# The two transfers that swap the halves of a pair's keys: begun by ScalarE behind its copy of the keys, or by SyncE in its line

## The chip, the cores and the metric

The kernel runs on one core of one Trainium2 chip. The metric is the device time of one execution in microseconds (us). Five engines matter here: TensorE (PE in the profile; PEld is its weight load), VectorE (DVE), ScalarE (ACT), GpSimd (POOL) and SyncE (SP, which issues transfers and computes nothing). Each works through its own instructions in order. A transfer (DMA) is begun by an instruction of one engine and carried out by DMA engines; a semaphore tells of its landing.

## What is computed

The reference is an attention with rotary positions, followed by a gated feed-forward layer and by a second one that chooses among eight experts. Only the attention is touched:

```python
def _attn_ref(q, k, v):                        # each 4 x 8 x 576 x 64, f32
    ...
    q_rot, k_rot = (rotate(q), rotate(k))
    scale = 1.0 / np.sqrt(D)
    scores = scale * np.matmul(q_rot, k_rot.transpose(0, 1, 3, 2))
    scores = scores - np.max(scores, axis=-1, keepdims=True)
    attn = np.exp(scores)
    attn = attn / (np.sum(attn, axis=-1, keepdims=True) + 1e-09)
    return np.matmul(attn, v).astype(np.float32)
...
x = attention, heads side by side: 2304 x 512
x = _moe_ref(x, ...)                           # (silu(x @ w_gate) * (x @ w_val)) @ w_out
return _moe2_ref(x, ...)                       # eight experts, one for each token, some tokens skipped
```

## The kernel before

The 32 heads are worked on as 16 pairs (0 to 15). A pair's queries are nine units of 128 rows (576 rows of two heads), so attention is 144 units, and one unit enters the pipeline in each step, or slot (`step`, L368). What a slot does stands in `ORDER`: the exponential of the unit before (`soft`, ScalarE), this unit's scores (`scores`, TensorE), part of an older unit's P.V product (`pv`), the copy of a finished product (`pv_out`, ScalarE, which also has SyncE store it to `xT`), the transposes of queries and keys of a coming pair (`qk_T`), the maximum (DVE), the transposes of the probabilities of the unit four slots back (`trans`), the jobs of this slot (`run_jobs`), and the copy of those transposed probabilities to SBUF (`his`: L282 on DVE for units 0, 2, 4, 6, L284 on ScalarE for the others).

The scores keep full f32 accuracy by splitting: of each number there is a high and a low part. `qk_T` transposes keys into the tile Ak, whose upper 64 partitions hold one part and whose lower 64 the other; ScalarE copies them out of PSUM in three groups (L186). The scores multiply Aq by Ak and by Bk, which is Ak with the two halves of its partitions exchanged. Bk is made in `swap` (L188): for pair 0 by TensorE, for the other 15 pairs by two transfers from SBUF to SBUF, 64 partitions of 4608 bytes each (L206, L207). The first product that reads Bk is the second matmul of the pair's unit 0 (L239).

When things are done is a table of slots relative to the pair's first unit (`AT`, `AT_FIRST`). The third group of keys is transposed and copied in slot -6 for pairs 2 to 15, and `swap` is a job of that same slot (for pair 1 it is slot -1). Slot -6 is the fourth slot of the pair before. In the slot's order the copy of the keys (L186) comes first, then the jobs with `swap`, then L284 for unit 8 of the pair before that one. In the next slot TensorE multiplies those probabilities by v (L318, `pv`), for which L284 must be done.

SyncE issues all other transfers of attention in the program's order, one after another: loads of q and k (L104), six loads of v (L116, L118), stores of x to `xT` (L337) and of the sums (L359). From slot 55 on it also issues, once per pair for eight pairs, what the next layer needs: a load of x (L560) and two to four loads of sums (L569). Weights for the next layer are loaded here and there (L457). The instructions' order on each engine is that of the program (`manual_schedule`), while the waits are put in by the framework.

Of the kernel before, what the change touches and what calls it, by code (L numbers as in the profile page):

```python
# [13 lines left out]
P = 128  # L14
G, R = 64, 9
# [3 lines left out]
def f32(ap):  # L19
    return ap.bitcast(F32)  # L20


class Attention:
# [164 lines left out]
    def swap(self, p):  # L188
        nc, st = self.nc, self.pairs[p]
        kb = self.p2.tile([P, 2 * S], F32R, tag="Bk", name=f"Bk_{p}")  # L190
        st["Bk"] = kb
        if p == 0:
            group = lambda t, g: t.rearrange("p (h r g) -> p h r g", h=2, r=R)[:, :, 3 * g:3 * g + 3]
            for g in range(3):
                if g < 2:
                    ps = self.psS.tile([P, 2, 512], F32, tag="S", name=f"swap{g}")[:, 0, :3 * P]
                else:
                    ps = self.psV.tile([P, 512], F32, tag="V", name=f"swap{g}")[:, :3 * P]
                ps = ps.rearrange("p (h r g) -> p h r g", h=2, r=3)
                nc.tensor.matmul(ps, self.swapr, group(st["Ak"], g), start=True, stop=True)  # L200
                if "b" + str(g) in self.FIRST_ON_DVE:
                    nc.vector.tensor_copy(group(kb, g), ps)
                else:
                    nc.scalar.copy(group(kb, g), ps)
            return
        nc.sync.dma_start(f32(kb[0:G]), f32(st["Ak"][G:P]))  # L206
        nc.sync.dma_start(f32(kb[G:P]), f32(st["Ak"][0:G]))  # L207

    def q_pad(self, p):
        nc, st = self.nc, self.pairs[p]  # L210
# [1292 lines left out]
```

## Time and profile before

| | before |
|---|---|
| median of 3 runs | 1042.92 us (1042.64 to 1045.4) |
| the profiled execution | 1042.63 us |
| its span in the trace | 1040.8 us |
| TensorE busy | 977.0 us (94%) |
| DVE busy | 559.6 us (54%) |
| ScalarE busy | 479.6 us (46%) |
| GpSimd busy | 442.4 us (43%) |

Attention takes roughly the first 330 us of the span. A share of the whole span says little about it, as ScalarE is far busier there than later; so the sums are read by stretch. In the timeline a row gives start, length, engine, line, operation and out<-in; in brackets stands the time for which the engine was idle before it, and what ended that. The rows of SyncE show the issuing instruction only, and not the transfer, which ends later. An x2 or x4 there is two or four issues in a row.

### The profile page before, as it was taken

How to read it: one execution, taken by the hardware profiler on the slowest of the kernel's cores; microseconds unless marked ns; L12 is line 12 of the kernel's file. 1: busy time of each engine (PE TensorE's matmuls, PEld its weight loads, DVE VectorE, ACT ScalarE, POOL GpSimd, SP SyncE). 2: the span in 40 equal slices, each digit the busy share in tenths (PEclk: the TensorE clock that was granted, in tenths of full speed). 3: DMA queues.
4: the chain of work that ended last, by engine and by line, in shares of the span. 5: the costliest groups of instructions: out<-in, count | busy, mean ns of one | idle time of the engine just before them, and what ended most of it. 6: DMA issues, size and time to landing. Idle time of an engine off the chain costs nothing. (4 is left out here: it accounts for less than half of the span.)

```text
span 1040.8 us, 16451 instructions
## 1 busy us (share of the span) xinstructions
PE 977.0 (94%) x5893; PEld 810.5 (78%) x5893; DVE 559.6 (54%) x962; ACT 479.6 (46%) x1041; POOL 442.4 (43%) x441
## 2 busy tenths in 40 slices
PE   5999998898989899999999999999999998998996
PEld 4787776676767878779999998999999876786643
DVE  6778776775856889883445233243245434225211
ACT  4888887786877333432343231232244314224232
POOL 6686777875830444455115315215216142112111
PEclk8999999998999999999999999999999999999999
DMA  5344455554532443413401211211222259506191
GB/s 175 91 135 126 134 154 146 148 137 130 126 85 101 140 122 101 121 57 92 137 23 54 77 46 31 76 47 31 73 89 62 72 139 395 223 31 215 32 371 57
DMA packets 81276, 119.80 MB, mean 115 GB/s; under 512 B 36469, under 2 KB 47365, under 8 KB 81168
## 3 DMA queue, kind: packets, MB, share of 16 engines
q1 hardware_dynamic: 77712, 110.01, 35.2%
q0 software_dynamic: 3456, 8.45, 2.8%
q8 instruction: 55, 0.90, 0.4%
q14 instruction: 53, 0.43, 0.1%
HBM read 87.73 MB, written 22.75 MB: 106 GB/s over the span
## 5 line engine op out<-in xcount | busy, mean ns | idle before, releaser
L614 POOL TENSOR_TENSOR hl<-h,hh 128x384 fp32r<-128x384 f32 x72 | 77.9, 1082 | 243.9 <-ACT hh L613 237.7
L251 DVE TENSOR_REDUCE nm<-S 128x1 f32<-128x576 f32 x144 | 108.3, 754 | 43.8 <-PE S L239 42.3
L259 ACT ACTIVATE P<-S,nm 128x576 f32<-128x576 f32 x144 | 107.2, 745 | 4.9 <-DVE nm L251 4.8
L613 ACT CAST hh<-h 128x384 fp32r<-128x384 f32 x72 | 37.0, 514 | 142.7 <-DVE h L612 142.7
L611 DVE TENSOR_TENSOR h<-g,h 128x384 f32<-128x384 f32 x72 | 40.0, 556 | 111.6 <-ACT h L610 111.6
L269 PE MATMUL T<-ident,P 128*128 128x128 f32 x576 | 90.9, 281 | 0.0
L239 PE MATMUL S<-Bk,Aq 128*128 128x288 f32 x256 | 74.5, 305 | 14.8 <-DMA Bk<-Ak 14.8
L627 PE MATMUL Y<-ohi,hl 128*128 128x512 f32 x216 | 85.9, 398 | 1.6 <-POOL hl L614 1.6
L318 PE MATMUL pv<-pt,rawv 128*64 128x384 f32 (+1 forms) x512 | 85.8, 438 | 1.5 <-ACT pt L284 1.4
L627 PE MATMUL Y<-ohi,hh 128*128 128x512 f32 x216 | 87.2, 404 | 0.0
L627 PE MATMUL Y<-olo,hh 128*128 128x512 f32 x216 | 85.3, 395 | 0.0
L239 PE MATMUL S<-Ak,Aq 128*128 128x288 f32 x256 | 83.0, 338 | 1.6 <-ACT P L259 1.6
L604 PE MATMUL g<-xa,ghi 128*128 128x384 f32 x216 | 75.6, 350 | 9.1 <-DVE h L611 8.6
L610 ACT ACTIVATE h<-g 128x384 f32<-128x384 f32 x72 | 35.1, 487 | 87.7 <-PE g L606 81.1
L606 PE MATMUL g<-xa,glo 128*128 128x384 f32 x216 | 72.4, 335 | 0.0
L606 PE MATMUL v<-xa,vlo 128*128 128x384 f32 x216 | 72.2, 334 | 0.0
L604 PE MATMUL v<-xa,vhi 128*128 128x384 f32 x216 | 72.1, 334 | 0.0
L269 PEld LDWEIGHTS T<-ident,P 128*128 128x128 f32 x576 | 64.6, 143 | 2.1 <-issue 1.2
L612 DVE TENSOR_TENSOR h<-v,h 128x384 f32<-128x384 f32 x72 | 40.2, 558 | 47.8 <-PE v L606 45.4
L239 PEld LDWEIGHTS S<-Bk,Aq 128*128 128x128 f32 x256 | 50.7, 198 | 16.6 <-issue 12.5
L282 DVE COPY pt<-T 128x512 f32<-128x512 f32 x64 | 44.2, 690 | 21.5 <-PE T L269 20.0
L239 PEld LDWEIGHTS S<-Ak,Aq 128*128 128x128 f32 x256 | 50.4, 197 | 6.7 <-issue 4.2
(268 smaller groups left out, 2533.3 us busy)
## 6 DMA issues: line engine op xcount, KB each, us to landing
wr_s<-in_moe_w_dram SPq DMA_DIRECT2D x46, 512.0 KB
xT<-x SPq DMA_DIRECT2D x32, 288.0 KB
x<-xT SPq DMA_DIRECT2D x24, 384.0 KB
Bk<-Ak SPq DMA_DIRECT2D x30, 288.0 KB
raw<-in_moe_w_gate_dram SPq DMA_DIRECT2D x12, 512.0 KB
raw<-in_moe_w_val_dram SPq DMA_DIRECT2D x12, 512.0 KB
raw<-in_moe_w_out_dram SPq DMA_DIRECT2D x12, 512.0 KB
wr<-in_moe_w_dram SPq DMA_DIRECT2D x10, 512.0 KB
```

The costliest lines, as they stand in the source:

```text
L239: nc.tensor.matmul(ps[:, c, :288], l, r[:, c * 288:(c + 1) * 288], start=(j == 0), stop=(j == len(ops) - 1))
L251: nc.vector.tensor_reduce(nm, st_u["S"], axis=AX.XY, op=ALU.max, negate=True)
L259: nc.scalar.activation(pt.rearrange("p (a b) -> p a b", a=2), st_u["S"], AF.Exp, bias=st_u["nm"], scale=1.0, accum_out=self.pairs[p]["l"][ ...
L269: nc.tensor.transpose(ps[:, kt * P:(kt + 1) * P], pt[:, kt * P:(kt + 1) * P], self.ident)
L282: self.nc.vector.tensor_copy(self.pt[:, :, cols], self.units[u]["T"])
L318: nc.tensor.matmul(ps[a * D:a * D + D, :n], st["raw"]["v"][:, h, 2 * third + a], self.pt[:, 2 * third + a, c0:c0 + n], start=(third == 0), ...
L604: nc.tensor.matmul(ps[m], wh[:, kt, cols], xh, start=(kt == 0), stop=False)
L606: nc.tensor.matmul(ps[m], wl[:, kt, cols], xh, start=False, stop=(kt == KT - 1))
L611: nc.vector.tensor_tensor(h, ps["g"], h, op=ALU.mult)
L612: nc.vector.tensor_tensor(h, ps["v"], h, op=ALU.mult)
L614: nc.gpsimd.tensor_tensor(hl, h, f32(hh), op=ALU.subtract)
L627: nc.tensor.matmul(self.acc[c][t], a[:, cols], b, start=(f == 0 and i == 0), stop=(f == FT - 1 and i == 2))
```

## The change

Both transfers that make Bk are issued by ScalarE and no longer by SyncE. Their place in the program, source, destination and size stay the same; for pair 0 nothing changes.

```diff
                 else:
                     nc.scalar.copy(group(kb, g), ps)
             return
-        nc.sync.dma_start(f32(kb[0:G]), f32(st["Ak"][G:P]))
-        nc.sync.dma_start(f32(kb[G:P]), f32(st["Ak"][0:G]))
+        nc.scalar.dma_start(f32(kb[0:G]), f32(st["Ak"][G:P]))
+        nc.scalar.dma_start(f32(kb[G:P]), f32(st["Ak"][0:G]))
```

## Rows read from the trace of the kernel before

**Rows 1.** Busy us (x instructions) by stretch, then PEclk, DMA share, GB/s:

```profile
52.40:143.40 91.00, 90.55 (x703) 70.02 (x701) 71.73 (x112) 77.94 (x193) 70.48 (x77) 1.00 0.51 135
143.40:310.80 167.40, 152.98 (x1121) 116.80 (x1122) 118.19 (x183) 125.41 (x310) 114.18 (x124) 0.95 0.49 131
```

**Rows 2.** Waits over the whole span: us in total, times, longest us:

```profile
PE S L239 <- DMA Bk<-Ak: 14.8, 6, 4.6
```

**Rows 3.** Timeline of TensorE: first products with Bk of pairs 12 and 14:

```profile
249.49 0.58 PE L239 MATMUL S<-Bk,Aq 128*128 128x288 f32 x1 [4.62 <-DMA Bk<-Ak]
...
291.20 0.37 PE L239 MATMUL S<-Bk,Aq 128*128 128x288 f32 x1 [2.77 <-DMA Bk<-Ak]
```

**Rows 4.** Timeline, pair 5: ScalarE's last copy of keys, and the swap:

```profile
95.33 0.48 ACT L186 CAST Ak<-M 128x384 fp32r<-128x384 f32 x1
...
95.84 0.54 SPq L206 DMA_DIRECT2D Bk<-Ak  x1
```

**Rows 5.** Timeline, pair 12: last copy of keys, and what follows:

```profile
233.48 0.48 ACT L186 CAST Ak<-M 128x384 fp32r<-128x384 f32 x1
233.89 0.59 ACT L284 COPY pt<-T 128x512 f32<-128x512 f32 x1
...
234.84 0.87 PE L318 MATMUL pv<-pt,rawv 128*64 128x384 f32 x4
```

**Rows 6.** Timeline of SyncE around the swap of pair 12, all issues:

```profile
221.92 0.54 SPq L337 DMA_DIRECT2D xT<-x  x1
222.56 2.14 SPq L457 DMA_DIRECT2D raw<-in_moe_w_val_dram  x1
225.38 0.33 SPq L104 DMA_DIRECT2D rawq<-in_q_dram  x1
225.81 1.36 SPq L116 DMA_DIRECT2D rawv<-in_v_dram  x2
227.22 1.27 SPq L118 DMA_DIRECT2D rawv<-in_v_dram  x1
228.53 2.78 SPq L116 DMA_DIRECT2D rawv<-in_v_dram  x2
232.72 0.59 SPq L118 DMA_DIRECT2D rawv<-in_v_dram  x1
234.69 0.38 SPq L560 DMA_DIRECT2D x<-xT  x1
235.39 2.79 SPq L569 DMA_DIRECT2D r<-rT  x4
238.28 0.55 SPq L337 DMA_DIRECT2D xT<-x  x1
238.94 0.42 SPq L359 DMA_DIRECT2D rT<-rr  x1
239.45 0.52 SPq L206 DMA_DIRECT2D Bk<-Ak  x1
240.02 0.59 SPq L207 DMA_DIRECT2D Bk<-Ak  x1
240.70 2.44 SPq L104 DMA_DIRECT2D rawk<-in_k_dram  x1
```

**Rows 7.** Waits of SyncE from 229 to 241 us, as rows 2:

```profile
SPq L118 <- DMA xT<-x: 1.4, 1, 1.4
SPq L560 <- DMA raw<-in_moe_w_val_dram: 1.3, 1, 1.3
...
SPq L569 <- DMA rawq<-in_q_dram: 0.3, 1, 0.3
```

**Rows 8.** Timeline: a copy by ScalarE, and TensorE that waited for it:

```profile
36.31 0.48 ACT L186 CAST Ak<-M 128x384 fp32r<-128x384 f32 x1 [0.40 <-PE M L177]
...
36.85 0.45 PE L177 MATMUL M<-identr,natk 128*128 128x128 f32 x3 [0.57 <-ACT Ak L186]
```

**Rows 9.** Timeline of POOL: the first work on the loaded x:

```profile
238.62 1.01 POOL L576 TENSOR_TENSOR x<-x 128x384 f32<-128x384 f32 x1 [5.10 <-DMA x<-xT]
```

## The prediction

> **What bounds the kernel now.** I read the sums by stretch first. In the stretch that covers five of attention's pairs without a long stall, TensorE is busy for 90.55 of 91.00 us, ScalarE for 77.94, at a granted clock of 1.00 [rows 1]: TensorE is the bound, and a pair costs 91.0 / 5 = 18.2 us. In the next eight pairs it is busy for 152.98 of 167.40 us at a clock of 0.95 [rows 1]: 14.4 us are idle, and the busy time is 153.0 - 8 x 18.1 = 8.2 us longer than at full clock. Then the list of waits: the one large wait of TensorE on a transfer is that of the scores for Bk, 14.8 us in six waits [rows 2]; the largest is 4.62 us, the last 2.77 us [rows 3]. All six lie at the first product of pairs 7, 8, 10, 11, 12 and 14. So there is something to win, but only in the second stretch.
>
> Why is Bk late there? Pair 5 shows the line as meant: ScalarE's copy of the keys ends at 95.33 + 0.48 = 95.81 and SyncE begins the first swap at 95.84 [rows 4]. In pair 12 the copy ends at 233.48 + 0.48 = 233.96 [rows 5], but SyncE comes to the swap at 239.45 only [rows 6], 5.5 us late; the second swap, begun at 240.02, lets TensorE go on at 249.49 [rows 3, 6], 9.5 us after its start. The reader is to see what held SyncE: at 232.72 a load of v waited 1.4 us for a store of xT, at 234.69 the load of x waited 1.3 us for a load of weights, at 235.39 the load of r waited for a load of q [rows 7]. These transfers share no data. Counting issues (x2 and x4 are two and four) shows the rule: each waits for the one eight places ahead of it. From the store at 221.92 to the load at 232.72, from the weights at 222.56 to x at 234.69, from q at 225.38 to the first r at 235.39 it is eight each time [rows 6]. Eight completion semaphores are handed out in turn, and a transfer doesn't start until the former owner of its semaphore has landed.
>
> **The change part by part.**
>
> *Removed: the wait for Bk.* Begun right behind the copy, the swap of pair 12 would start 5.5 us earlier, more than the stall of 4.62. If nothing holds it, all 14.8 us go [rows 2].
>
> *Added: two issues in ScalarE's order.* No issue by ScalarE stands in the trace; the nearest rows are the same two on SyncE: 0.57 us from the first's start to the second's (239.45 to 240.02), and 0.59 for the second, 1.16 in all [rows 6]. Behind them on ScalarE stands the copy of the transposed probabilities (L284), and for that TensorE waits with the P.V product L318. Today L284 starts at 233.89, 0.07 before the copy of the keys has ended, because nothing separates the two; it ends at 234.48, and L318 starts at 234.84, 0.36 later [rows 5]. This distance of 0.36 us stands at 13 of the 15 swaps. A released TensorE starts 0.06 after the copy's end (36.31 + 0.48 = 36.79, 36.85) [rows 8], which leaves 0.30 of slack. With the change L284 is later by 0.07 (lost overlap) + 0.03 (start behind the copy, as SyncE's in pair 5) + 1.16 = 1.26 us, so TensorE stalls 1.26 - 0.30 = 0.96 us per pair. That isn't made up, as TensorE is the bound there. Bounds: nothing, if ScalarE hands the issue on while it works; 0.46, if each takes the 0.33 of the cheapest load; and with a second issue held like the load of k behind the swaps today (2.44) [rows 6], 0.07 + 0.03 + 0.57 + 2.44 - 0.30 = 2.8. I take 0.96, the row of the same transfer.
>
> *Added: the turn of eight, now on ScalarE.* Nothing in the trace shows whether an issue by ScalarE keeps its place in that turn. The turn runs through every kind of SyncE's transfers without a break, so it goes by the program's order, not by tile or line; I take it that the swaps keep their places. Then the first swap of pair 12 waits for the eighth before it, the load of v issued at 232.72, and the second for the load of x issued at 234.69. The load of x ends a wait of POOL at 238.62 [rows 9], 3.9 us after its issue; by the same 3.9 (an estimate) the load of v lands at 236.6. ScalarE stands still from 233.96 to 238.6, issues the second swap, 0.59, and is free at 239.2. L284 comes 239.2 - 233.89 = 5.3 us later, TensorE stalls 5.3 - 0.3 = 5.0 us. Today's stall of this pair is 4.62. Queued behind the waiting instruction are L284 and then the next exponential, with DVE, POOL and TensorE behind these. So in the loaded stretch the stall moves from pair 12's first product to an L318 some ten us earlier, and is no shorter: the same line of SyncE (store of xT, load of v, load of x) sets both. For pairs 7 to 14 I put gain against cost at nothing, with bounds of -3 us (waits of ScalarE that come out shorter, as each delay gives SyncE's line time) and +6 us (0.96 in pairs 9 and 13, which have no stall today, and a place or two of the turn that is late in the others too).
>
> *Taken from SyncE:* two issues, 1.16 us a pair, and the load of k behind them can start earlier. TensorE waits for no other transfer [rows 2], so this is worth nothing directly.
>
> *Sum.* Pairs 1 to 6 and 15 have no stall to lose and pay 0.96 each: 7 x 0.96 = 6.7 us. Pairs 7 to 14: 0. The profiled run took 1042.63 us (span 1040.8), so 1042.6 + 6.7 = 1049.3 us; the profiled run is 0.3 under the median of 1042.92, so I leave it there. What follows attention begins with TensorE's last product and moves as a whole.
>
> **The rivals.**
>
> *The swaps are outside the turn of eight (faster).* If ScalarE's issues have semaphores of their own, it doesn't wait. The price is 15 x 0.96 = 14.4 us, the gain 14.8, and where the stalls go the clock need not fall: up to 8.2 us. 1042.6 + 14.4 - 14.8 - 8.2 = 1034.0 us. For it: the turn is seen on SyncE alone. Against it: it spares no kind of transfer. A rule of the Trainium skill bears on this side too (DMA: Bandwidth & Descriptors, "Queues, rings and completion order"): each issuing engine has rings of its own, and a DMA engine takes turns between rings. By it Bk would no longer stand behind the store of xT; the 9.5 us of pair 12 would shrink, and the same 14.8 us go, so it adds nothing to the sum. Chance 0.14.
>
> *ScalarE's issue is held (much slower).* Behind the swaps SyncE's load of k takes 2.44 us, the load of q of the same size 0.33 [rows 6]: something holds an issue for some 2 us when much is queued. If that hits the second swap on ScalarE, it adds 2.44 - 0.59 = 1.85 in each of the seven free pairs, 13 us: 1062 us; more if the loaded pairs pay as well. It decides from the point where SyncE's issues and ScalarE's meet. The Trainium skill has a rule for this (Perfetto Trace Analysis, "DMA Instruction — HWDGE"): the two issuing sequencers share one descriptor generator, locked for one issue at a time, and the lock wait counts in the instruction's time. Against it: the swaps themselves take 0.52 and 0.59 right behind the large store of xT [rows 6]. Chance 0.10.
>
> *Cheap issue, or an exchange that favours the change (even).* With 0.33 an issue the seven pairs cost 7 x 0.46 = 3.2 us; with the lower bound of the loaded pairs (-3) it is about nothing: 1042.6 to 1045.8, say 1043.5 us. Here falls also the case that the change does nothing: the swap starts no earlier and ScalarE has slack that I don't see. Chance 0.21.
>
> **How the numbers follow.** Forecast 1049.3 us, chance 0.55; its own range by the bounds above is 1042.6 + 3.7 to 1042.6 + 12.7, so 1046 to 1055. With the rivals the range is 1035 to 1060: it leaves out about half of each outer case. About 0.3%, 3.1 us, is what a measurement can tell here. Slower by more than that: 0.50 of the forecast and 0.10 of the held issue, 0.60. Same: 0.05 of the forecast and 0.17 of the even case, 0.22. Faster: 0.14 and 0.04 of the even case, 0.18.
>
> **What would show it.** Right: the 14.8 us of waits for Bk are gone; in their place L318 waits for ScalarE's L284, some 1 us in pairs 2 to 6 and 2 to 5 us in pairs 8, 10, 12 and 14; ScalarE's issues take 0.5 to 0.6 us, and in those pairs lie behind waits for a transfer of SyncE's. The period of pairs 2 to 6 goes from 18.1 to 19.1 us, that of the loaded ones stays near 21. Wrong: no wait of ScalarE on transfers (then the first rival, and a shorter second stretch), or issues of 2 us and more (the second), or L318 without a wait in pairs 2 to 6 (cheap issue).

## The result, and the profile after

The changed kernel takes 1054.55 us (median of 4 runs, 1052.12 to 1057.38) against 1042.78 us for the kernel before: a ratio of 1.011 with a 95% interval of 1.009 to 1.013. It is slower, as forecast, but by 11.8 us and not by 6.7. The profiled execution took 1057.38 us with a span of 1055.6 us, which is 14.8 us more than the span of before.

The page's busy times of after come first. TensorE is busy for about as long as before (979.7 us against 977.0), so 12.1 of the 14.8 us are idle time.

```profile
PE 979.7 (93%) x5893; PEld 812.8 (77%) x5893; DVE 558.5 (53%) x962; ACT 480.1 (45%) x1041; POOL 441.9 (42%) x441
```

The two stretches of [rows 1] follow, in the same columns (stretch, its length, busy us of PE, PEld, DVE, ACT and POOL with instructions, PEclk, DMA share, GB/s):

```profile
59.30:156.10 96.80, 90.65 (x703) 70.10 (x702) 71.16 (x111) 77.78 (x192) 69.81 (x77) 1.00 0.47 130
156.10:323.80 167.70, 150.57 (x1122) 115.40 (x1121) 119.88 (x184) 126.09 (x312) 115.46 (x124) 0.97 0.47 129
```

In the free stretch TensorE's work is the same (90.65 us against 90.55), and it lasts 5.8 us longer. In the loaded one 14.4 us of idle time became 17.1, the busy time fell by 2.4 us at the better clock (0.97 against 0.95), and the length stayed. TensorE's large waits in attention (20 to 330 us; total, times, longest) answer to [rows 2]:

```profile
PE pv L318 <- ACT pt L284: 23.9, 14, 3.4
PE S L239 <- DMA Bk<-Ak: 3.1, 1, 3.1
```

All six waits for Bk of before are gone, and fourteen waits of P.V for ScalarE's copy stand in their place, one in each of pairs 2 to 15. One wait for Bk is new. It is that of pair 1, which had none.

Every kernel below is read in the same way, by the start of the first product with Bk (L239, in the timeline of TensorE) of pairs 2, 7 and 15. The first column holds the start-up as well: TensorE's first matmul starts 9.8 (before) to 11.5 us (e12) into the span.

| kernel | until pair 2 | pair 2 to 7 | pair 7 to 15 | after that | span |
|---|---|---|---|---|---|
| before | 52.4 | 91.0 | 167.4 | 730.0 | 1040.8 |
| after | 59.3 | 96.8 | 167.7 | 731.8 | 1055.6 |
| after, again (e9) | 58.6 | 96.5 | 170.2 | 729.5 | 1054.8 |
| pair 1 by SyncE (e1) | 53.3 | 97.1 | 172.4 | 729.5 | 1052.2 |
| pair 1 by SyncE, again (e10) | 53.3 | 97.5 | 168.4 | 730.0 | 1049.2 |
| pair 1 at its copy (e8) | 54.0 | 96.5 | 169.0 | 729.2 | 1048.7 |
| behind L284 (e2) | 53.1 | 93.3 | 167.3 | 728.9 | 1042.6 |
| pairs 7 to 14 alone (e3) | 53.1 | 92.1 | 167.6 | 729.7 | 1042.5 |
| before, store split (e4) | 52.4 | 90.4 | 146.8 | 727.8 | 1017.4 |
| after, store split (e5) | 61.3 | 99.5 | 157.9 | 728.2 | 1046.9 |
| e1, store split (e6) | 53.3 | 97.5 | 156.0 | 732.1 | 1038.9 |
| e2, store split (e7) | 53.4 | 93.1 | 149.3 | 727.5 | 1023.3 |
| by GpSimd (e11) | 52.5 | 91.9 | 163.9 | 732.5 | 1040.9 |
| by GpSimd, store split (e12) | 53.2 | 90.4 | 146.8 | 730.4 | 1020.9 |

The first two lines say where the 14.8 us came from: 6.9 until pair 2 (0.8 of it a later first matmul, 10.57 us against 9.81), 5.8 to pair 7, 0.3 to pair 15 and 1.8 behind. The last is no more than what this column varies by (727.5 to 732.5).

**Pairs 2 to 6: the working of the prediction, seen.** The timeline of pair 5 (start, length, engine, line; in brackets the idle time before and what ended it) answers to [rows 4]:

```profile
104.91 0.48 ACT L186 CAST Ak<-M 128x384 fp32r<-128x384 f32 x1
...
105.42 0.47 ACTq L206 DMA_DIRECT2D Bk<-Ak  x1
...
105.93 0.61 ACTq L207 DMA_DIRECT2D Bk<-Ak  x1
...
106.58 0.59 ACT L284 COPY pt<-T 128x512 f32<-128x512 f32 x1 [1.19 <-PE S L239]
...
107.22 0.54 PE L318 MATMUL pv<-pt,rawv 128*64 128x384 f32 x2 [0.89 <-ACT pt L284]
```

The first issue starts 0.03 us behind the copy, the two take 0.47 and 0.61 us, and TensorE stalls 0.89 us. The releaser named for L284 had long been done; it is the two issues that fill the 1.19 us. In pair 4, which has a stall of 1.62 us, an issue waits as well:

```profile
85.17 0.49 ACT L186 CAST Ak<-M 128x384 fp32r<-128x384 f32 x1
86.42 0.47 ACTq L206 DMA_DIRECT2D Bk<-Ak  x1
86.93 0.61 ACTq L207 DMA_DIRECT2D Bk<-Ak  x1
87.58 0.59 ACT L284 COPY pt<-T 128x512 f32<-128x512 f32 x1 [1.92 <-DMA rawv<-in_v_dram]
```

The copy ends at 85.66 and the swap starts at 86.42. What let it go is the landing of a load of v: by its semaphore, SyncE's load begun at 79.42 landed at 86.35. Pair 6 is the same (begun at 118.16, landed at 125.14, stall 1.68 us).

**Pair 12: the wait on SyncE's transfers, seen.** ScalarE's rows answer to [rows 5], SyncE's to [rows 6]:

```profile
247.92 0.49 ACT L186 CAST Ak<-M 128x384 fp32r<-128x384 f32 x1
249.62 0.47 ACTq L206 DMA_DIRECT2D Bk<-Ak  x1
251.57 0.47 ACTq L207 DMA_DIRECT2D Bk<-Ak  x1
252.08 0.59 ACT L284 COPY pt<-T 128x512 f32<-128x512 f32 x1 [3.67 <-DMA r<-rT]
252.72 0.65 PE L318 MATMUL pv<-pt,rawv 128*64 128x384 f32 x2 [3.37 <-ACT pt L284]
...
243.19 1.79 SPq L116 DMA_DIRECT2D rawv<-in_v_dram  x2
246.78 0.60 SPq L118 DMA_DIRECT2D rawv<-in_v_dram  x1
248.09 0.39 SPq L560 DMA_DIRECT2D x<-xT  x1
248.78 2.85 SPq L569 DMA_DIRECT2D r<-rT  x4
```

The copy ends at 248.41. The first swap starts 1.2 us later, when the load of v begun at 243.19 has landed (249.55 by its semaphore), and the second another two us later, when the first of the loads of r has (251.55). Neither has any data in common with the swap; the wait is for the shared semaphore. In the trace SyncE's and ScalarE's transfers carry the same eight semaphores (100 to 107), and the two that ScalarE waited for had these two loads as owners. Over attention the list of waits (total, times, longest) gives ScalarE these, and the first line holds pairs 4 and 6 too:

```profile
ACT pt L284 <- DMA rawv<-in_v_dram: 9.3, 4, 2.8
ACT pt L284 <- DMA r<-rT: 3.7, 1, 3.7
ACT pt L284 <- DMA x<-xT: 1.8, 1, 1.8
```

**Pair 1: what the prediction missed.** Its last copy of keys and its swap:

```profile
27.23 0.48 ACT L186 CAST Ak<-M 128x384 fp32r<-128x384 f32 x1
...
31.82 0.51 ACTq L206 DMA_DIRECT2D Bk<-Ak  x1
32.36 0.60 ACTq L207 DMA_DIRECT2D Bk<-Ak  x1
...
36.56 0.38 PE L239 MATMUL S<-Bk,Aq 128*128 128x288 f32 x1 [3.11 <-DMA Bk<-Ak]
```

The copy ends at 27.71 and ScalarE comes to the swap 4.1 us later. For pair 1 the swap is a job of slot -1, while the last copy of keys lies in slot -3. SyncE, with nothing else to do, ran ahead to that job and waited for the copy alone: before, its swap started at 27.80. ScalarE has the slots between to work through. So Bk is 3.1 us late, just where the pipeline begins, and the clock falls behind the stall: between 36.5 and 48.0 us the granted clock is 0.70, a mixture of the 2.4 and the 1.2 GHz level (6.8 us at the lower one), against 1.00 in the same window of before.

### The profile page after: what moved, and what is told of

It reads as the page before. It is cut to its first block, busy times and chain, and to the rows that moved or that the text cites. A ratio compares the mean times of both kernels' runs of the same rounds, so it can differ in the third digit from the quotient of the medians.

```text
span 1055.6 us, 16380 instructions
## 1 busy us (share of the span) xinstructions
PE 979.7 (93%) x5893; PEld 812.8 (77%) x5893; DVE 558.5 (53%) x962; ACT 480.1 (45%) x1041; POOL 441.9 (42%) x441
## 5 line engine op out<-in xcount | busy, mean ns | idle before, releaser
L259 ACT ACTIVATE P<-S,nm 128x576 f32<-128x576 f32 x144 | 107.3, 745 | 7.9 <-DVE nm L251 6.9
L318 PE MATMUL pv<-pt,rawv 128*64 128x384 f32 (+1 forms) x512 | 85.0, 433 | 25.4 <-ACT pt L284 25.3
L239 PE MATMUL S<-Ak,Aq 128*128 128x288 f32 x256 | 82.8, 338 | 1.8 <-ACT P L259 1.5
L239 PE MATMUL S<-Bk,Aq 128*128 128x288 f32 x256 | 74.0, 303 | 3.1 <-DMA Bk<-Ak 3.1
L318 PEld LDWEIGHTS pv<-pt,rawv 128*64 128x64 f32 x512 | 28.6, 137 | 43.8 <-ACT pt L284 29.0
L284 ACT COPY pt<-T 128x512 f32<-128x512 f32 x80 | 47.0, 587 | 29.0 <-DMA rawv<-in_v_dram 9.3
```

The lines of the kernel that those rows point to most:

```text
L239: nc.tensor.matmul(ps[:, c, :288], l, r[:, c * 288:(c + 1) * 288], start=(j == 0), stop=(j == len(ops) - 1))
L259: nc.scalar.activation(pt.rearrange("p (a b) -> p a b", a=2), st_u["S"], AF.Exp, bias=st_u["nm"], scale=1.0, accum_out=self.pairs[p]["l"][ ...
L284: self.nc.scalar.copy(self.pt[:, :, cols], self.units[u]["T"])
L318: nc.tensor.matmul(ps[a * D:a * D + D, :n], st["raw"]["v"][:, h, 2 * third + a], self.pt[:, 2 * third + a, c0:c0 + n], start=(third == 0), ...
```

## The experiments

**e1: pair 1 back to SyncE, pairs 2 to 15 by ScalarE.**

```diff
-        nc.scalar.dma_start(f32(kb[0:G]), f32(st["Ak"][G:P]))
-        nc.scalar.dma_start(f32(kb[G:P]), f32(st["Ak"][0:G]))
+        eng = nc.sync if p == 1 else nc.scalar
+        eng.dma_start(f32(kb[0:G]), f32(st["Ak"][G:P]))
+        eng.dma_start(f32(kb[G:P]), f32(st["Ak"][0:G]))
```

> The swap of pair 1 goes back to SyncE; pairs 2 to 15 stay with ScalarE. Theory: pair 1's swap is a job of slot -1, two slots behind its copy of the keys; SyncE began it at the copy's end, ScalarE only when its own order came to it, 4 us later, and this cost a stall of 3.1 us and 6.8 us at half clock (another 3.4). So this kernel gains 5 to 6.5 us on the changed one: ratio to before 1.006, about 1048.5 us. Rival: pair 1 costs what the other pairs cost (1 us) and the surplus over my forecast lies in the later pairs: then 1053 us, ratio 1.010.

Measured: 1053.79 us, a ratio of 1.0092 (1.0065 to 1.0119), 5 us above the number given and close to the rival's 1053. In its trace the wait for Bk is gone and pair 2 begins at 53.3 instead of 59.3 us, as expected, but the stretch from pair 7 to 15 took 172.4 us. The edit changes no instruction of that stretch. So this time and that of after, 0.8 us apart and not taken side by side, could not price pair 1; both were run again side by side as e9 and e10.

**e2: pair 1 by SyncE, the other swaps by ScalarE behind L284.** The job only notes the two tiles, and `swap_out`, called at the end of `step`, has ScalarE issue both transfers.

```diff
-        nc.scalar.dma_start(f32(kb[0:G]), f32(st["Ak"][G:P]))
-        nc.scalar.dma_start(f32(kb[G:P]), f32(st["Ak"][0:G]))
+        if p == 1:
+            nc.sync.dma_start(f32(kb[0:G]), f32(st["Ak"][G:P]))
+            nc.sync.dma_start(f32(kb[G:P]), f32(st["Ak"][0:G]))
+        else:
+            self.swap_last = (kb, st["Ak"])
...
+        self.swap_out()
```

> As e1, but ScalarE begins the two transfers of pairs 2 to 15 at the slot's end, behind its copy L284, for which TensorE waits, instead of ahead of it. Theory (the price in the free pairs is L284 coming later): L318 no longer waits in pairs 2, 3, 5 and 15 (0.9 each now), and next in line is the exponential, which has over 1 us of room; about 5 us less than e1, 1043 to 1045 us. The loaded pairs keep waits of ScalarE on SyncE's transfers, shorter by 0.6 to 1 us each at most. Rival (ScalarE has no room anywhere, so each us of issue is a us of TensorE): the wait moves to the next exponential and the time is that of e1, 1048 to 1049.

Measured: 1045.06 us, 1.0019 (1.0001 to 1.0037), 8.7 us less than e1 beside it, and as expected. P.V hardly waits any more; TensorE's waits in attention are now

```profile
PE S L250 <- ACT P L270: 15.2, 13, 3.1
...
PE pv L329 <- ACT pt L295: 0.2, 1, 0.2
```

(L250, L270, L295 and L329 are L239, L259, L284 and L318 of the other kernels.) The free stretch is 3.8 us shorter than in e1, 93.3 against 97.1. This shows that most of what the change costs there, 3.8 of the 6.1 us that e1 takes more than before, is the place of the issues ahead of L284. In the loaded stretch the waits on semaphores delay the next exponential instead, and the scores wait for it; it lasts 167.3 us, as before.

**e3: only pairs 7 to 14 by ScalarE**, where before had its stalls (`eng = nc.scalar if 7 <= p <= 14 else nc.sync`).

> ScalarE begins the swaps of pairs 7 to 14 alone, SyncE those of the others. Theory (one line of SyncE sets both the wait for Bk and ScalarE's wait): even with before, 1041 to 1046 us, with the 14.8 us of waits for Bk replaced by 15 to 18 us of waits of L318. Rival (removing the late start in the loaded pairs is worth its 14.8 us, and the loss of the changed kernel lies in the free pairs): 1030 to 1035 us.

Measured: 1044.15 us, 1.001 (0.9994 to 1.0026): even, as expected. The loaded stretch lasts 167.6 us against 167.4. This is the exchange at nothing of the prediction, measured alone. The waits that stand in place of the 14.8 us (L319 and L285 are L318 and L284) are longer than the 15 to 18 expected:

```profile
PE pv L319 <- ACT pt L285: 19.7, 8, 4.0
```

**e4: the kernel before, with the store of xT in two.** In before, loads on SyncE wait for a store of xT to land; their total, times and longest over pairs 7 to 15 (140 to 325 us) are

```profile
SPq L560 <- DMA xT<-x: 9.2, 4, 2.5
...
SPq L118 <- DMA xT<-x: 5.0, 3, 1.9
```

The semaphores' increments in the trace put a store's landing 8.5 to 12.4 us behind its issue. Its destination has the outermost dimension 2 (two heads of 64 rows), and its packets in the trace (11 to 12 of 93 ns in each 0.5 us of its middle part) keep 11.5 x 93 / 500 = about two DMA engines busy. Its semaphore rises in three steps, one about 1 us after the issue and two at the end, where that of a swap rises in sixteen. The experiment writes each head by a transfer of its own, whose outermost dimension is 64; nothing else changes, and SyncE issues all swaps.

```diff
-            nc.sync.dma_start(self.xT[:, row:row + D, b * S:(b + 1) * S], st["x"])
+            for a in range(2):
+                nc.sync.dma_start(self.xT[a, row:row + D, b * S:(b + 1) * S], st["x"][a * D:(a + 1) * D])
```

> The kernel before with SyncE's swaps, and the store of x to xT as two transfers of 64 partitions instead of one whose outer dimension is 2. Theory: the store is the slow member of the turn (8.5 to 12 us to its landing), because it is spread over two DMA engines only, so all that shares these engines and all that waits for its semaphore is late; spread like the swap it lands in 4 us or less, SyncE is no longer late, and the waits for Bk go: 14.8 us and up to 8 us of clock, against 32 more issues on SyncE: 1020 to 1030 us. Rival (the eight semaphores bind by count, whatever each transfer takes): one more transfer per store makes SyncE later: 1045 us or more.

Measured: 1019.98 us, 0.9783 (0.9756 to 0.9811), faster than both kernels. The two stretches of [rows 1]:

```profile
52.40:142.70 90.30, 90.30 (x701) 70.01 (x701) 71.07 (x111) 77.33 (x192) 70.61 (x76) 1.00 0.55 139
142.70:289.60 146.90, 146.34 (x1123) 112.36 (x1122) 119.98 (x184) 125.56 (x313) 115.66 (x124) 1.00 0.57 148
```

The loaded stretch is 20.5 us shorter: 13.9 us of idle time are gone, and 6.6 of busy time at the better clock. Issues of the page (times, KB each, median us to landing), and the one wait left for Bk:

```profile
xT<-x SPq DMA_DIRECT2D x64, 144.0 KB, 2.5
...
Bk<-Ak SPq DMA_DIRECT2D x30, 288.0 KB, 4.1
...
PE S L239 <- DMA Bk<-Ak: 0.2, 1, 0.2
```

A store lands 2.5 us after its issue, and SyncE has no wait for one. In pair 12 its swap starts at 225.67 us and TensorE needs Bk at 234.72, without a stall. So the late Bk of before was the slow store's doing, in two ways that this run doesn't part. In pair 12 the swap started 5.5 us behind the copy of the keys, and here 1.7. And of its second transfer's sixteen increments fourteen came within 6.6 us of the issue and the last two only after 8.9 and 9.3, a tail of two that the swaps behind a store show in pairs 2 to 15 of before; here all sixteen come within 3.9 us. The Trainium skill has the rule (DMA: Bandwidth & Descriptors, "Why a DMA increments its semaphore by 16 and not by 1"): the slowest dimension of both sides decides on how many engines a transfer runs, the largest number up to 16 that divides both; by it two engines carried the store of before, and 16 each half. The times to landing here, 8.5 to 12.4 against 2.5 us, agree, and so do the steps of the semaphore: each half's rises in sixteen.

**e5, e6, e7: after, e1 and e2, each with the split store.**

> The changed kernel (ScalarE begins all swaps) with the store of x to xT split as in the run before. Theory (two prices: the turn of eight through slow stores, and the issue ahead of L284): the stores land in 2.5 us, so ScalarE no longer waits for SyncE's transfers, but L318 still waits 0.9 us in each of pairs 2 to 15, 14 x 0.9 = 12.6, and pair 1 costs its 3.1 us and 3.4 of clock: 1020 + 12.6 + 6 = 1038 us, ratio to before 0.995. Rival (the whole loss of the change came from waiting on SyncE's late transfers): 1020 to 1024 us.

> As the one before, but pair 1's swap begun by SyncE. Theory: the difference to it is the price of pair 1 alone, 5 to 6.5 us: 1032 us, ratio 0.990. Rival (pair 1 is worth nothing, as the run with the unsplit store says in its medians, 0.8 us): 1037 us, within 1.5 of the one before.

> Split store, pair 1's swap begun by SyncE, the others by ScalarE behind its copy L284. Theory: with neither wait of ScalarE nor a late L284 this is the time of SyncE's swaps with the split store, 1019 to 1022 us; the issue alone costs nothing. Rival (1.1 us of ScalarE per pair costs TensorE something wherever it stands): 1024 to 1032 us. Rival on the other side (SyncE's freed 1.2 us are worth something): under 1018 us.

Measured on one chip: e5 1045.15 us, 1.0006 (0.9984 to 1.0027); e6 1040.09, 0.9966 (0.9948 to 0.9984); e7 1025.78, 0.9831 (0.9805 to 0.9857). The differences hold what was looked for: pair 1 costs e5 - e6 = 5.1 us, and the place ahead of L284, with the waits that come with it, e6 - e7 = 14.3 us, in fourteen pairs now that no stall of before hides any of it. The absolute times of e5 and e6 were missed by 7 and 8 us, and e7 lies in the range of its rival (1024 to 1032) and not at 1019 to 1022. Behind L284 the issues are cheaper but not free: against e4 the table gives e7 2.7 us more from pair 2 to 7, where one issue was held (below), and 2.5 to pair 15, and in e7 the scores wait for the exponential (L250 and L270 as in e2):

```profile
PE S L250 <- ACT P L270: 4.5, 5, 1.3
```

Waits of TensorE and ScalarE in e6 (its L285 and L319 are L284 and L318):

```profile
PE pv L319 <- ACT pt L285: 16.7, 15, 1.9
...
ACT pt L285 <- DMA r<-rT: 5.8, 3, 2.2
...
ACT pt L285 <- DMA x<-xT: 2.0, 1, 2.0
```

I had taken it that with the store landing early nothing would hold a swap. But the owners of its semaphores are then the loads of r and x that SyncE began a few us before, and these need their time to land: the stalls of pairs 7 to 14 are 0.89 to 1.87 us, not 0.9 each. In pairs 2 to 6 they are 0.88 to 0.89: the 0.7 and 0.8 us more of pairs 4 and 6 in after came with the slow store too. Also, one issue of ScalarE in e5 (pair 5) takes 2.02 us, with a stall of 2.30 us behind it:

```profile
107.36 0.47 ACTq L206 DMA_DIRECT2D Bk<-Ak  x1
107.87 2.02 ACTq L207 DMA_DIRECT2D Bk<-Ak  x1
```

e7 has one of 1.78 us, and there are two shorter ones, 1.28 us in e5 (pair 4) and 1.15 us in e10 (pair 5). SyncE issues nothing beside the first two, so what holds them isn't shown.

**e8: after, with the swap of pair 1 in the slot of its last copy of keys** (`"swap": -1` becomes `-3` in `AT_FIRST`), all by ScalarE.

> The changed kernel with pair 1's swap as a job of slot -3, where its last copy of keys stands, instead of slot -1; ScalarE begins all swaps, the store is the old one. Theory (place, not engine): the first product with Bk of pair 1 no longer waits 3.1 us, and pair 2 begins 5 to 6 us earlier, as with SyncE. For the whole: 1049 us if the run with pair 1 on SyncE gave its gain back by chance in the loaded stretch (172.4 us there, 167.3 to 167.7 in four others); 1053 to 1054 us if the loaded stretch gives it back whenever pair 1 is repaired.

Measured: 1052.80 us, 1.009 (1.0064 to 1.0116). The swap now starts at 28.27 us, 0.66 behind the copy, TensorE doesn't wait for Bk, and pair 2 begins at 54.0 instead of 59.3 us. So it was the slot, and not the engine's cost of an issue, that made pair 1 dear. The median fell by only 2 to 3 us against after and e9, which were not taken beside it, less than the trace's 5.3; its profiled execution, 1050.6, was the fastest of its six. So the whole lies nearer to the 1053 to 1054 us of the expectation than to 1049, while the loaded stretch of its trace (169.0 us) doesn't show the gain given back.

**e9 and e10: after and e1 again, side by side.**

> The changed kernel once more, beside the next run on the same chip, to size pair 1's price with the old store. From the loaded stretch of its first profile: 167.7 us from the first product with Bk of pair 7 to that of pair 15; 1053 to 1056 us.

> The changed kernel with pair 1's swap on SyncE, once more. Theory A (the loaded stretch takes what it gets by chance, 167 to 173 us): 3 to 6 us faster than the changed kernel beside it. Theory B (an earlier arrival is given back in the loaded stretch, since transfers set its pace): 0 to 2 us faster, and the loaded stretch longer by 3 to 5 us in this profile too.

Measured: 1055.62 us, 1.0096 (1.0065 to 1.0127), and 1051.12, 1.0073 (1.0046 to 1.0101). Pair 1 costs 4.5 us by the medians and 5.3 until pair 2 by the table (0.35 of it a later first matmul). Both times are as expected, e10 by theory A; its loaded stretch, 168.4 us against 170.2 in e9, is not longer, as theory B would have it.

**e11 and e12: the swaps by GpSimd** (`nc.gpsimd.dma_start`, both), with the store of before and with the split one.

> GpSimd begins all swaps, the store is the old one. GpSimd's transfers have semaphores of their own, outside the turn of eight, and GpSimd isn't ahead of any wait of TensorE within a slot. Theory (the turn and the place ahead of L284 are the two prices of ScalarE): no waits of L318, the swap of the loaded pairs starts near the copy of the keys, and the waits for Bk go: 1028 to 1036 us. Rival (Bk is late because DMA engines are full, whoever begins it): the waits for Bk stay at 10 us or more, 1040 us and up. Rival (GpSimd's issue or its place in line costs the rotary work): waits of TensorE on natk or Aq, 1036 to 1045 us.

> The swaps issued by GpSimd as in the run before, and the store of xT cut in two by its outer dimension. Theory A: what kept the GpSimd version at 1042 was the slow store alone (17 waits of ScalarE's copy of x for it, 29.2 us); with the store split they are gone, TensorE has no wait over 0.6 us in attention, the stretch from pair 7 to pair 15 goes from 163.9 to about 147 us, and the time is that of the split alone, 1018 to 1023 us. Rival: GpSimd's two issues, about 1.1 us per pair, or a hold on them, delay its own work on the keys and cost TensorE: 1026 us or more, with TensorE waiting for something made by GpSimd or for Bk.

Measured: e11 1042.18 us, 0.9979 (0.9959 to 0.9999), missing the expected 1028 to 1036. GpSimd's transfers carry eight semaphores of their own in the trace (111 to 118). TensorE waits 0.6 us for Bk and 2.6 for L284, and yet the loaded stretch is only 3.5 us shorter. Waits of TensorE, and of ScalarE's copy of a finished product:

```profile
PE pv L318 <- ACT x L333: 10.2, 8, 2.4
...
ACT x L333 <- DMA xT<-x: 29.2, 17, 3.7
```

The copy waits for a buffer from which the store still reads. In before this wait was 4.9 us in five times. With Bk out of the way, the slow store is the next to be late. e12 gave 1023.49 us, 0.9806 (0.9767 to 0.9844), half a us above the range that I had set; both waits are gone, and the two stretches last 90.4 and 146.8 us, those of e4 to 0.1. So GpSimd's two issues (0.58 and 0.52 us on average) cost nothing in these stretches, where its engine isn't waited for. With the split store the whole price of the swaps on ScalarE, e5 against e12, is 8.1 + 9.1 + 11.1 = 28.3 us in these two executions and 21.7 by the medians, as e5's execution was slower than its median.

## Why the prediction was right or wrong, point by point

- **The wait for Bk goes.** Right in the pairs that it named: 14.8 us in six waits became none there.
- **0.96 us in each free pair.** Right where no issue waits: 0.84 to 0.89 us in pairs 2, 3, 5 and 15. It is the lost overlap, two issues and a slack of 0.30, as worked out; e2, where these pairs have no wait of L318, shows the place ahead of L284 as the cause.
- **The swaps keep the shared semaphores.** Right, so the first rival falls: ScalarE waits for loads of v, r and x (pair 12 above). In pair 14 their owners were a load of v and the load of x, as worked out for pair 12; in pair 12 the second was a load of r instead, and the stall 3.37 us and not 5.0. Counting eight back along SyncE's line alone is no longer exact once two engines issue. The stall of pair 14 was 1.5 us, below the 2 to 5 named, and pair 13, free of a stall before, got one of 2.6.
- **Pairs 7 to 14 an exchange at nothing.** Right within its bounds of -3 and +6: +0.3 us in after, 1.001 in e3. It is idle time against clock: 2.7 us more idle, 2.4 us less busy. But the +0.3 is the lowest of five executions: after, e9, e1, e10 and e8, with the same swaps there, took 167.7 to 172.4 us, on average 2.1 more than the one execution of before.
- **Held issues of 2 us (second rival).** Not in after, where the longest of the 30 issues takes 0.80 us; once each in e5 and e7, so the chance was not zero. What I set against this rival, swaps of 0.52 and 0.59 us behind the store, was not the whole trace of before: in pair 11 the second swap took 2.92 us. SyncE's issues of over 1 us, though, fell from 32 to 10 in attention, and those of the load of k behind the swaps from 2.4 to 0.3 to 1.3 us. The Trainium skill's rule of one descriptor generator locked for one issue at a time (Perfetto Trace Analysis, "DMA Instruction — HWDGE") would have both engines hold each other; the traces show little of that. Beside the 0.80 lies an issue of SyncE, which makes some 0.3 us; SyncE's store at 293.55 us took 1.00 us instead of mostly 0.53 to 0.55 with a whole issue of ScalarE inside it; but its load of r at 206.73 has one inside it too and took the usual 0.60.
- **Cheap issues (third rival).** No: the two take 0.47 + 0.61 = 1.08 us, close to the 1.16 that SyncE's rows gave, and not twice 0.33.
- **Wrong: pair 1 at 0.96 us.** This is the step that failed. I wrote that pairs 1 to 6 and 15 pay 0.96 each, and had pair 1's slot (-1) from the table of slots, but read it only as another place for the same price. For a swap whose slot lies behind its copy's, the price isn't the issue time but the way from the copy to that slot in ScalarE's own order: 4.1 us here, of which 3.1 come out as a stall, and behind it TensorE runs at the lower clock for 6.8 us. Until pair 2 after loses 6.0 us against e1 by both. By the medians of runs side by side it is 4.5 (e9, e10) and 5.1 us (e5, e6).
- **Mis-sized: pairs 4 and 6.** I gave the free pairs no wait on a semaphore at all. A load of v owns it there as well, and adds 0.7 and 0.8 us.
- **The sum.** In the profiled execution the forecast's +1.9 us until pair 2 was 6.9 (6.2 without the later first matmul), +3.8 to pair 7 was 5.8, +1.0 behind that 0.3, and 1.8 are the part after attention. The median lies 2.8 us under that execution. With pair 1 at 4.5 to 5.1 instead of 0.96, and 1.5 for pairs 4 and 6, the sum would have been 1042.6 + 6.7 + 3.5 to 4.1 + 1.5 = 1054.3 to 1054.9 us, where 1054.55 was measured. That is closer than the terms are known: by runs that were not side by side pair 1 costs 0.8 (after, e1) to 2.8 us (e9, e8), which would make it 1050.6 to 1052.6 and leave the rest to other terms, such as the loaded stretch. The forecast's own range (1046 to 1055) holds the measured time by luck: its room upward was meant for pairs 7 to 14, while in the profiled execution 7.0 us of what came over the forecast lay before pair 7, most of them in pair 1.

What stays open: the loaded stretch took 167.7, 170.2, 172.4, 168.4 and 169.0 us in five executions of kernels that issue the same work there in the same order. The transfers whose semaphores the swaps wait for are the same in all five; what varies is when they land. L318's stalls in that stretch sum to 15.9 to 21.1 us and the time at the lower clock to 10.2 to 17.1 us. What sets this in one execution was not found, and a median of few runs can't price an edit under 3 us unless both kernels run side by side.

## What to carry to other kernels

A transfer that is moved to a computing engine starts when that engine's order comes to it, not when its data is ready, and whatever stands behind it waits for its issue and for its semaphore: look at each place where it is issued, not at the repeated one alone. When a line of transfers is late, look for what makes it late before taking something out of it: here one store on few DMA engines did, and splitting it gave 2.2%, where each move of the swaps alone was even or worse. And when one late thing is removed, ask which wait on the same cause comes next.

## What was not expected of the hardware

An issue by GpSimd (0.52 to 0.58 us) costs its engine about what one costs ScalarE (0.47 to 0.61 us), so the engine should be chosen by who waits for it. A stall of 3.1 us of TensorE at pair 1 was followed by the lower clock (0.70 over the next 11.5 us), while stalls of 0.89 to 1.68 us in each of pairs 3 to 7 left it at 1.00 for 96.8 us. The length of one stall doesn't decide it: in the loaded stretch of after the clock fell behind those of 2.35, 2.45 and 3.37 us (pairs 10, 8 and 12), and not behind those of 2.63 and 2.59 (pairs 11 and 13). And swaps begun by ScalarE took their share of the DMA engines beside the slow store: the store issued next to a swap landed after 10.0 to 11.8 us instead of 8.4 to 9.1, and in pairs 5 to 14 the second transfer of a swap after 3.9 to 9.0 instead of 9.1 to 9.4. The Trainium skill's rule that the prediction weighed (DMA: Bandwidth & Descriptors, "Queues, rings and completion order") agrees with this taking of turns. It gained nothing, as ScalarE's waits ahead of the issue, and no longer the swap's flight, lay on the path.
